# A fused attention and feed-forward kernel: 12 hash rows copied by DMA for the attention mask, a Horner form read from PSUM, and a weight conversion with work moved off VectorE

## The chip, the cores and the metric

The kernel runs on one core of one Trainium2 chip. The metric is the device time of one execution in microseconds; less is better. Engines: TensorE (PE in the profile; PEld are its weight loads), VectorE (DVE), ScalarE (ACT), GpSimd (POOL), and SyncE (SP), which here only issues DMAs. Each engine runs its own instructions strictly in order. A tile framework with a list scheduler decides that order from the program and from its own estimates, so a change of one operation can move others.

## The reference

```python
# 1: attention, 2 batches x 8 heads, 768 tokens, head size 64; a token sees only keys of its own hash bucket
q_bits = (einsum('bhsd,dk->bhsk', q, proj) > 0)      # 6 bits each; k_bits likewise
mask = q_bucket[..., :, None] == k_bucket[..., None, :]
scores = where(mask, q @ k.T / 8, -1e9); attn = softmax(scores); x = attn @ v
# 2: feed-forward "a", 1536 tokens, 512 -> 2048 -> 512, float64 weights
h = x @ w_in
g = (a0 + a1 h + a2 h^2 + a3 h^3) / (1 + |b0||h| + |b1| h^2 + 1e-6)
x = g @ w_out
# 3: 8 experts "b", 512 -> 1024 -> 512, float32, each with relu, weighted by a Sinkhorn gate P
out = sum_e P[:, e] * (relu(x @ w1[e]) @ w2[e])
```

## The kernel before

Float32 products run as float32r passes: an operand is split into a high part (hi) and a low part (lo = a - hi), and hi*hi + hi*lo + lo*hi is summed in PSUM.

**Attention** loops over 16 heads, and in each over three pairs of 128-query tiles. Per tile `scores` does two products (L259, and L260 with the stacked operands `a2`, `b2`) into PSUM; VectorE copies them out with a row minimum (L266); ScalarE takes the exponential (L267); GpSimd divides by the row sum (L274). Later iterations transpose (L288), split the result (`pth` by ScalarE, `ptl` by VectorE, both tiles from L99 and L102) and multiply with the values (L303). The next head is prepared meanwhile: `prep_head_a` splits q, k and v on GpSimd, transposes them (L221) and copies them out on ScalarE as `a1`, `b1`; VectorE copies halves of them into `a2` and `b2` (L223, L224). `prep_head_b` computes hash values (L236) and turns them into bits (L237, VectorE). `prep_head_c` multiplies the bits with a sign code (L246), and ScalarE turns the result into 64 mask rows of `a2` and of `b2` (L247, L248).

**Feed-forward "a"** has 48 steps of 512 tokens by 128 hidden units. A step has 12 matmuls into PSUM (`gemm1`, tile `h`, L343), the rational function (`activate`, L358 to L370, then `gh` and `gl`), and, three steps later, 12 matmuls of `gemm2` (L391). The temporary tiles `tu`, `tw`, `tq`, `tr` have two buffers each, `gh` and `gl` four, and PSUM has four banks for `h`. The float64 weights of 16 hidden tiles come as pairs of 32-bit words. `narrow` turns 512 columns of them into float32 (L162 to L169; twice for each of the 16 tiles), and a split follows (ScalarE hi, GpSimd lo). Ten of these 32 calls run during attention, 22 during feed-forward "a".

**Experts "b"** have 192 steps of the same 24 matmuls with a short activation (L374 ScalarE, L375 VectorE), which the change leaves alone.

DMAs are issued by SP, in order; q, k and v of head i + 2 are loaded when head i has been split.

Of the kernel before, what the change touches and what calls it, by code (L numbers as in the profile page):

```python
# [31 lines left out]
def kernel(  # L32
# [194 lines left out]
    hs = {}  # L227

    def prep_head_b(i):
        """hash bits of the queries (rows 0:NB) and keys (rows 64:64+NB)"""  # L230
        a1, a2, b1_, b2, _ = st[i]
        bits = ap.tile([P, S], BF16, tag="bits", bufs=1, name="bits")
        for n0, n1 in COLS:
            hp = bank("hp")[:, 0:n1 - n0]
            for j, r in enumerate((a1, a1, b1_, b1_)):
                pe.matmul(hp, lhsT=pjr[:, j], rhs=r[:, n0:n1], start=j == 0, stop=j == 3)  # L236
            dve.tensor_scalar(bits[:, n0:n1], hp, 0.0, None, ALU.is_gt)  # L237
        hs[i] = bits

    def prep_head_c(i):  # L240
        """bucket rows: 0 for a query's own bucket and -1 elsewhere, BIG for a key's own bucket and 0 elsewhere"""
        a1, a2, b1_, b2, _ = st[i]
        bits = hs.pop(i)
        for n0, n1 in COLS:
            dp = bank("dp")[:, 0:n1 - n0]
# [374 lines left out]
```

## Time and profile before

| | us |
|---|---|
| median of 3 runs | 1775.38 (1774.77 to 1777.22) |
| profiled execution, first to last instruction (span) | 1771.8 |
| what the median has beyond that span | 3.6 |
| attention, 0 to about 316 | 316 |
| feed-forward "a", 316 to about 706 | 390 |
| gate and experts "b", 706 to the end | 1066 |

The span is the profile's time from the first to the last instruction of one execution. The start and the end of an execution lie around it. Stage borders are read from the first `h` matmuls of a kind on TensorE, and stages overlap there by some microseconds.

### The profile page before, as it was taken

The page shows a single profiled execution, that of the slowest core. Times are in us where ns is not written, and L with a number is a line of the kernel's source. Part 1 is how long each engine was busy: PE and PEld are TensorE (multiplying, and loading weights), DVE is VectorE, ACT ScalarE, POOL GpSimd, SP SyncE. Part 2 cuts the span into 40 slices and gives each one's busy share as a digit, 9 for nine tenths or more (in the row PEclk, how much of TensorE's full clock was granted, in tenths as well). Part 3 has the DMA queues.
Part 4 walks back from the last instruction along what each step waited for, and adds up shares of the span by engine and source line. Part 5 has one row for each costly group of instructions (what it writes and reads, how often), then busy time and mean ns, then how long its engine had stood idle before and what let it go on. Part 6 is the DMA issues. An engine that isn't in the chain of part 4 may idle for free.

```text
span 1771.8 us, 19718 instructions
## 1 busy us (share of the span) xinstructions
PE 1631.5 (92%) x7716; PEld 1340.4 (76%) x7716; DVE 887.9 (50%) x1414; ACT 607.1 (34%) x1101; POOL 694.8 (39%) x660
## 2 busy tenths in 40 slices
PE   6898989776776788999999999999999999999998
PEld 5777778655665666788888888888888888888887
DVE  8999999899999988521112111111211111121112
ACT  5888888556555556111111111111111111111110
POOL 6777775666666674302303303304204204105100
PEclk9999999897888899999999999999999999999999
DMA  4111110011111110100200201101101101101001
...
DMA packets 46062, 64.20 MB, mean 36 GB/s; under 512 B 3473, under 2 KB 34193, under 8 KB 45969
## 3 DMA queue, kind: packets, MB, share of 16 engines
...
## 4 chain that ended last, share of the span: by engine, by line
PE 65%; DVE 22%; ACT 6%; issue 4%; POOL 2%; SPq 0%; DMA 0%; DVEq 0%; POOLq 0%
PE acc L391 30%; PE h L343 29%; DVE tr L369 3%; DVE tq L368 3%; DVE tu L370 2%; PE av L303 2%; ACT e L267 2%; DVE tq L363 2%; DVE gl L102 1%; PE pt L288 1%; DVE e L266 1%; DVE ptl L102 1%; DVE u L165 1%; DVE c L162 1%; ACT pth L99 1%
## 5 line engine op out<-in xcount | busy, mean ns | idle before, releaser
L375 DVE SCALAR_TENSOR_TENSOR gl<-h,gh 128x512 fp32r<-128x512 f32 x192 | 132.7, 692 | 809.5 <-ACT gh L374 809.4
L343 PE MATMUL h<-x2h,w 128*128 128x512 f32 x1536 | 504.3, 389 | 0.0
L391 PE MATMUL acc<-w,gh 128*128 128x512 f32 x1536 | 473.7, 389 | 0.6 <-DVE part L403 0.6
L374 ACT ACTIVATE gh<-h 128x512 fp32r<-128x512 f32 x192 | 114.8, 598 | 915.2 <-PE h L343 915.1
L391 PEld LDWEIGHTS acc<-w,gh 128*128 128x128 f32 x1536 | 288.1, 188 | 60.7 <-DVE part L403 1.0
L343 PEld LDWEIGHTS h<-x2h,w 128*128 128x128 f32 x1536 | 288.1, 188 | 59.7
L93 POOL TENSOR_SCALAR w<-ra 128x512 fp32r<-128x512 f32 x64 | 41.5, 649 | 719.1 <-PE acc L391 719.1
L391 PE MATMUL acc<-w,gl 128*128 128x512 f32 x768 | 299.1, 389 | 0.0
L343 PE MATMUL h<-x2l,w 128*128 128x512 f32 x768 | 298.8, 389 | 0.0
L391 PE MATMUL acc<-gh,w 128*128 128x512 f32 x384 | 149.1, 452 | 79.2 <-DVE part L403 24.8
L391 PEld LDWEIGHTS acc<-w,gl 128*128 128x128 f32 x768 | 144.3, 188 | 29.9
L343 PEld LDWEIGHTS h<-x2l,w 128*128 128x128 f32 x768 | 144.3, 188 | 29.8
L391 PEld LDWEIGHTS acc<-gh,w 128*128 128x128 f32 x384 | 85.0, 222 | 106.6 <-ACT gh L99 40.4
L343 PE MATMUL h<-xh,w 128*128 128x512 f32 x384 | 127.4, 395 | 0.0
L274 POOL TENSOR_SCALAR e<-e,rs 128x768 f32<-128x768 f32 x96 | 101.4, 1067 | 43.0 <-DVE rs L272 41.1
L366 POOL TENSOR_TENSOR tu<-tu,tsq 128x512 f32<-128x512 f32 x48 | 77.6, 1618 | 69.4 <-ACT tu L360 65.9
L391 PE MATMUL acc<-gl,w 128*128 128x512 f32 x192 | 86.9, 453 | 13.0 <-DVE gl L102 13.0
L102 DVE TENSOR_TENSOR ptl<-pt,pth 128x512 fp32r<-128x512 f32 x144 | 94.6, 683 | 5.5 <-ACT pth L99 4.2
L288 PE MATMUL pt<-idr,e 128*128 128x128 f32 x576 | 83.9, 277 | 10.2 <-ACT b L248 5.4
L267 ACT ACTIVATE e<-e,nm 128x768 f32<-128x768 f32 x96 | 90.4, 941 | 7.2 <-DVE e L266 6.1
L266 DVE TENSOR_SCALAR_CACHE_REDUCE e<-s 128x768 f32<-128x768 f32 x96 | 90.6, 945 | 1.4 <-PE s L260 1.0
L99 ACT ACTIVATE pth<-pt 128x512 fp32r<-128x512 f32 x144 | 81.2, 598 | 16.5 <-PE pt L288 14.8
...
## 6 DMA issues: line engine op xcount, KB each, us to landing
ra<-in_moe_w_dram SPq DMA_DIRECT2D x32, 512.0 KB, 3.4
rb<-in_moe_w_dram SPq DMA_DIRECT2D x32, 512.0 KB, 4.2
ra<-in_moe_w_in_dram SPq DMA_DIRECT2D x16, 512.0 KB, 3.7
rb<-in_moe_w_out_dram SPq DMA_DIRECT2D x16, 512.0 KB, 3.4
qkv<-in_q_dram SPq DMA_DIRECT2D x16, 192.0 KB, 2.4
qkv<-in_k_dram SPq DMA_DIRECT2D x16, 192.0 KB, 2.5
qkv<-in_v_dram SPq DMA_DIRECT2D x16, 192.0 KB, 3.2
...
```

What stands on the lines that cost most here:

```text
L99: act.activation(o, src, AF.Copy)
L102: dve.tensor_tensor(lo, src, hi.bitcast(F32), ALU.subtract)
L266: dve.tensor_scalar(e[j], s[:, 0:S], -1.0 / D ** 0.5, None, ALU.mult, ALU.min, accum_out=nm)
L267: act.activation(e[j], e[j], AF.Exp, bias=nm, scale=-1.0, accum_out=rs[:, j:j + 1])
L274: pool.tensor_scalar(e[j], e[j], rs[:, j:j + 1], 0.0, ALU.mult, ALU.add)
L288: pe.transpose(pt[:, c, j * P:(j + 1) * P], e[j][:, cc * P:(cc + 1) * P], idf)
L343: pe.matmul(hps, lhsT=w[:, c], rhs=x[:, c], start=m == 0, stop=m == 3 * KC - 1)
L366: pool.tensor_tensor(tu, tu, tsq, ALU.mult)
L368: dve.scalar_tensor_tensor(tq, tq, dbias, tr, ALU.add, ALU.mult)
L374: act.activation(gh, hps, AF.Relu)
L375: dve.scalar_tensor_tensor(gl, hps, 0.0, gh.bitcast(F32), ALU.max, ALU.subtract)
L391: pe.matmul(o, lhsT=l[:, js], rhs=r, start=f == 0 and m == 0, stop=f == nf - 1 and m == 2)
```

## The change

Attention: the sign code, its product and `prep_head_c` go. For each token a matmul now gives 12 hash values (the six with both signs), a VectorE operation turns them into 0/1 rows for queries and 0/2^60 rows for keys, and DMAs copy these 12 rows, and also the 64-row halves that VectorE copied, into `a2` and `b2`. A key whose six bits agree contributes 6 * 2^60 in the second product, which now contracts over 76 rows. The factor -1/8 moves from L266 into the copy of `a1`.

Feed-forward: the polynomial and the denominator are evaluated by Horner's rule with `h` read from PSUM by three VectorE operations; both GpSimd operations and the square go, and `gl` moves from VectorE to GpSimd. In `narrow`, the first bit operation of VectorE becomes an absolute value on ScalarE and the clamp moves to GpSimd; tile `u` has one buffer in place of two.

```diff
     def narrow(bits):
-        u = conv.tile([P, n], I32, tag="u", name="u")
+        u = conv.tile([P, n], I32, tag="u", bufs=1, name="u")
-        dve.tensor_scalar(ci, hw, 0x7FFFFFFF, None, ALU.bitwise_and)
-        dve.tensor_scalar(c, c, F64_LOW, F64_HIGH, ALU.max, ALU.min)
+        act.activation(c, hw.bitcast(F32), AF.Abs)
+        pool.tensor_scalar(c, c, F64_HIGH, F64_LOW, ALU.min, ALU.max)
...
-        for src, dst in ((sq, a1), (sk, b1_)):
+        for src, dst, scale in ((sq, a1, -1.0 / D ** 0.5), (sk, b1_, 1.0)):
...
-                act_copy(dst[:, n0:n1], tp[:, 0:n1 - n0].bitcast(F32))
-        dve.tensor_copy(a2[0:64], a1[0:64].bitcast(F32))
-        dve.tensor_copy(b2[0:64], b1_[64:128].bitcast(F32))
+                act.activation(dst[:, n0:n1], tp[:, 0:n1 - n0].bitcast(F32), AF.Copy, scale=scale)
+        sp.dma_start(a2[0:64].bitcast(F32), a1[0:64].bitcast(F32))
+        sp.dma_start(b2[0:64].bitcast(F32), b1_[64:128].bitcast(F32))
...
-            dve.tensor_scalar(bits[:, n0:n1], hp, 0.0, None, ALU.is_gt)
+            dve.tensor_scalar(bits[QROW:KROW + 2 * NB, n0:n1], hp[QROW:], thr[QROW:KROW + 2 * NB, 0:1],
+                              thr[QROW:KROW + 2 * NB, 1:2], ALU.is_ge, ALU.mult)
+        sp.dma_start(a2[QROW:QROW + 2 * NB].bitcast(F32), bits[QROW:QROW + 2 * NB].bitcast(F32))
+        sp.dma_start(b2[QROW:QROW + 2 * NB].bitcast(F32), bits[KROW:KROW + 2 * NB].bitcast(F32))
...
-    def prep_head_c(i):
-            pe.matmul(dp, lhsT=codeT, rhs=bits[:, n0:n1], start=True, stop=True)
-            act.activation(a2[64:128, n0:n1], dp[0:64], AF.Sign, bias=obias[0:64])
-            act.activation(b2[64:128, n0:n1], dp[64:128], AF.Relu, bias=obias[64:128], scale=BIG)
...
-            pe.matmul(s[:, n0:n1], lhsT=a2[:, cs], rhs=b2[:, n0:n1], start=False, stop=True)
+            pe.matmul(s[:, n0:n1], lhsT=a2[0:QROW + 2 * NB, cs], rhs=b2[0:QROW + 2 * NB, n0:n1],
+                      start=False, stop=True)
...
-            act.activation(tsq, hps, AF.Square)
-            act.activation(tq, hps, AF.Abs, scale=cb[:, 0:1])
+            act.activation(tw, hps, AF.Abs, scale=cb[:, 1:2])
             act.activation(tu, hps, AF.Identity, scale=na[:, 3:4], bias=na[:, 2:3])
-            act.activation(tw, hps, AF.Identity, scale=na[:, 1:2], bias=na[:, 0:1])
-            dve.scalar_tensor_tensor(tq, tsq, b1, tq, ALU.mult, ALU.add)
+            dve.scalar_tensor_tensor(tw, tw, ab[:, 0:1], hps, ALU.add, ALU.mult)
+            act.activation(tq, tw, AF.Abs)
             act.activation(tr, tq, AF.Ln, bias=dbias)
             act.activation(tr, tr, AF.Exp, scale=-1.0)
-            pool.tensor_tensor(tu, tu, tsq, ALU.mult)
-            pool.tensor_tensor(tu, tu, tw, ALU.add)
+            dve.tensor_tensor(tu, tu, hps, ALU.mult)
+            dve.scalar_tensor_tensor(tu, tu, na[:, 1:2], hps, ALU.add, ALU.mult)
             dve.scalar_tensor_tensor(tq, tq, dbias, tr, ALU.add, ALU.mult)
-            dve.scalar_tensor_tensor(tr, tq, -2.0, tr, ALU.add, ALU.mult)
-            dve.tensor_tensor(tu, tu, tr, ALU.mult)
+            dve.scalar_tensor_tensor(tu, tu, na[:, 0:1], tr, ALU.add, ALU.mult)
+            dve.scalar_tensor_tensor(tu, tq, -2.0, tu, ALU.add, ALU.mult)
             act_copy(gh, tu)
-            dve_lo(gl, tu, gh)
+            pool_lo(gl, tu, gh)
```

In the changed kernel the new VectorE lines of a step are L357, L361, L362 (these read `h` from PSUM) and L363, L364, L365; ScalarE's are L355 (`tw`), L356 (`tu`), L358 (`tq`), L359 and L360 (`tr`), and L102 (`gh`); those of `narrow` are L166 (ScalarE), L167 (GpSimd), L168, L169, L171, L172 (VectorE), L173 (GpSimd).

VectorE, in the middle of feed-forward "a", before: about one step with a part of a weight conversion (the numbers after the names tell buffers of different steps apart).

```order
L102 TENSOR_TENSOR gl_4312<-tu_4313,gh_4311 128x512
L369 SCALAR_TENSOR_TENSOR tr_4351<-tq_4350,tr_4351 128x512
L363 SCALAR_TENSOR_TENSOR tq_4398<-tsq_4397,b1_303,tq_4398 128x512
L370 TENSOR_TENSOR tu_4347<-tu_4347,tr_4351 128x512
L164 TENSOR_SCALAR c_4663<-c_4663 128x512
L162 TENSOR_SCALAR c_4674<-rb_4438 128x512
L165 SCALAR_TENSOR_TENSOR u_4664<-ra_4437,c_4663 128x512
L102 TENSOR_TENSOR gl_4346<-tu_4347,gh_4345 128x512
L368 SCALAR_TENSOR_TENSOR tq_4398<-tq_4398,dbias_308,tr_4399 128x512
```

The same engine and place in the changed kernel, a little over one step.

```order
L365 SCALAR_TENSOR_TENSOR tu_4242<-tq_4244,tu_4242 128x512
L361 TENSOR_TENSOR tu_4288<-tu_4288,h_4259 128x512
L171 TENSOR_SCALAR c_4432<-u_4433 128x512
L362 SCALAR_TENSOR_TENSOR tu_4288<-tu_4288,na_297,h_4259 128x512
L172 SCALAR_TENSOR_TENSOR c_4432<-rb_3861,c_4432 128x512
L357 SCALAR_TENSOR_TENSOR tw_4360<-tw_4360,ab_294,h_4332 128x512
L363 SCALAR_TENSOR_TENSOR tq_4290<-tq_4290,dbias_299,tr_4291 128x512
L364 SCALAR_TENSOR_TENSOR tu_4288<-tu_4288,na_297,tr_4291 128x512
L361 TENSOR_TENSOR tu_4359<-tu_4359,h_4332 128x512
L365 SCALAR_TENSOR_TENSOR tu_4288<-tq_4290,tu_4288 128x512
```

Where every operation read two tiles from SBUF (or one from SBUF alone), operations that read `h` now stand between those; `gl` is gone from here, and the first product of the next step (`tu_4359`) stands ahead of the last one of this step (`tu_4288`).

ScalarE at the same place in the changed kernel.

```order
L358 ACTIVATE tq_4290<-tw_4289 128x512
L102 ACTIVATE gh_4240<-tu_4242 128x512
L359 ACTIVATE tr_4291<-tq_4290,dbias_299 128x512
L356 ACTIVATE tu_4359<-h_4332,na_297 128x512
L360 ACTIVATE tr_4291<-tr_4291 128x512
L355 ACTIVATE tw_4404<-h_4376,cb_285 128x512
```

The first `tu` of a step (`tu_4359`) takes the buffer of the step two before it (`tu_4242`), which GpSimd's new `gl` operation is the last to read; behind it stands L360, the exponential of the step between them.

SP during attention in the changed kernel, from one head's loads to the next one's; before, there were only the three loads per head, and a weight load in some of them.

```order
L117 DMA qkv_1590<-in_q_dram 128x384
L117 DMA qkv_1590<-in_k_dram 128x384
L117 DMA qkv_1590<-in_v_dram 128x384
L227 DMA a2_1595<-a1_1594 64x768
L228 DMA b2_1597<-b1_1596 64x768
L242 DMA a2_1595<-bits_1684 12x768
L243 DMA b2_1597<-bits_1684 12x768
```

Four copies per head stand behind the loads of two heads later; in some heads a 512 KB weight load stands ahead of the last two of them.

## Rows read from the trace of the kernel before

**Rows 1.** The page: its span and its first part, busy time of each engine.

```profile
span 1771.8 us, 19718 instructions
PE 1631.5 (92%) x7716; PEld 1340.4 (76%) x7716; DVE 887.9 (50%) x1414; ACT 607.1 (34%) x1101; POOL 694.8 (39%) x660
```

**Rows 2.** Busy us of each engine by stage: attention, feed-forward "a", experts.

```profile
60.00:290.00 230.00, 206.24 (x1459) 178.63 (x1458) 221.46 (x463) 197.02 (x399) 171.53 (x193) 0.99 0.15 45
...
316.00:706.00 390.00, 297.64 (x1141) 230.42 (x1140) 363.93 (x409) 228.14 (x379) 243.10 (x162) 0.87 0.11 36
...
760.00:1772.00 1012.00, 1007.30 (x4444) 833.73 (x4443) 194.45 (x281) 110.63 (x185) 208.08 (x224) 1.00 0.09 31
```

**Rows 3.** VectorE by line, 60 to 290 us: busy us, mean ns, idle before.

```profile
L102 DVE TENSOR_TENSOR ptl<-pt,pth 128x512 fp32r<-128x512 f32 x111 | 73.0, 682 | 2.1 <-ACT pth L99 1.0
...
L224 DVE CAST b<-b 64x768 fp32r<-64x768 f32 x12 | 12.9, 1071 | 0.8 <-ACT b L99 0.5
...
L223 DVE CAST a<-a 64x768 fp32r<-64x768 f32 x12 | 8.7, 723 | 0.0
```

**Rows 4.** VectorE by line, 0 to 316 us: the clamp of the weight conversion.

```profile
L163 DVE TENSOR_SCALAR c<-c 128x512 f32<-128x512 f32 x10 | 6.4, 641 | 0.0
```

**Rows 5.** Timeline of one head's mask: start us, us, engine, line.

```profile
171.70 0.99 DVE L237 TENSOR_SCALAR bits<-hp 128x512 bf16<-128x512 f32 x2
...
179.02 0.47 ACT L248 ACTIVATE b<-dp,obias 64x256 fp32r<-64x256 f32 x1
...
179.01 0.40 PE L260 MATMUL s<-b,a 128*128 128x512 f32 x1
```

**Rows 6.** DMA issues, 150 to 175 us: KB each, median us to landing.

```profile
rb<-in_moe_w_out_dram SPq DMA_DIRECT2D x1, 512.0 KB, 5.0
qkv<-in_q_dram SPq DMA_DIRECT2D x1, 192.0 KB, 2.3
```

**Rows 7.** By line, 316 to 706 us: VectorE, GpSimd, ScalarE.

```profile
L369 DVE SCALAR_TENSOR_TENSOR tr<-tq,tr 128x512 f32<-128x512 f32 x47 | 54.0, 1150 | 0.4
...
L403 DVE TENSOR_TENSOR part<-part,acc 128x512 f32<-128x512 f32 x32 | 20.3, 676 | 0.0
...
L366 POOL TENSOR_TENSOR tu<-tu,tsq 128x512 f32<-128x512 f32 x47 | 75.9, 1615 | 69.4 <-ACT tu L360 65.9 <-DVE gl L102 3.5
...
L169 POOL TENSOR_TENSOR c<-u,c 128x512 f32<-128x512 f32 x22 | 38.8, 1763 | 48.5 <-DVE c L168 48.5
...
L360 ACT ACTIVATE tu<-h,na 128x512 f32<-128x512 f32 x47 | 36.6, 778 | 14.1 <-DVE gl L102 14.1
...
L365 ACT ACTIVATE tr<-tr 128x512 f32<-128x512 f32 x48 | 30.0, 626 | 0.5
```

**Rows 8.** Timeline of VectorE and GpSimd in feed-forward "a": start us, us, engine, line.

```profile
420.68 1.81 DVE L363 SCALAR_TENSOR_TENSOR tq<-tsq,b,tq 128x512 f32<-128x512 f32 x1
...
420.65 1.29 POOL L366 TENSOR_TENSOR tu<-tu,tsq 128x512 f32<-128x512 f32 x1 [0.44 <-ACT tu L360]
...
426.04 0.74 DVE L368 SCALAR_TENSOR_TENSOR tq<-tq,dbias,tr 128x512 f32<-128x512 f32 x1
426.70 0.68 DVE L165 SCALAR_TENSOR_TENSOR u<-ra,c 128x512 int32<-128x512 int32 x1
427.30 0.68 DVE L369 SCALAR_TENSOR_TENSOR tr<-tq,tr 128x512 f32<-128x512 f32 x1
427.90 0.41 DVE L167 TENSOR_SCALAR c<-u 128x512 int32<-128x512 int32 x1
428.24 0.68 DVE L370 TENSOR_TENSOR tu<-tu,tr 128x512 f32<-128x512 f32 x1
```

**Rows 9.** By line, 800 to 1700 us (experts): VectorE and GpSimd.

```profile
L375 DVE SCALAR_TENSOR_TENSOR gl<-h,gh 128x512 fp32r<-128x512 f32 x166 | 114.8, 692 | 729.2 <-ACT gh L374 729.2
...
L96 POOL TENSOR_TENSOR w<-ra,w 128x512 fp32r<-128x512 f32 x56 | 72.2, 1290 | 0.0
L93 POOL TENSOR_SCALAR w<-ra 128x512 fp32r<-128x512 f32 x56 | 35.1, 626 | 712.7 <-PE acc L391 712.7
```

More of the change, by code (lines that the diff above doesn't have):

```diff
@@ L25 @@
 BIG = 2.0 ** 60
+QROW, KROW = 64, 96
+F_BELOW = 2.0 ** -126
+F_MIN = 2.0 ** -126 * (1.0 + 2.0 ** -23)
 F64_LOW = float.fromhex("0x1p-15")
@@ L221, in prep_head_a @@
                     pe.transpose(tp[:, c * P - n0:(c + 1) * P - n0], src[:, c], idr)
[L222 to L224 removed]
+                act.activation(dst[:, n0:n1], tp[:, 0:n1 - n0].bitcast(F32), AF.Copy, scale=scale)
+        sp.dma_start(a2[0:64].bitcast(F32), a1[0:64].bitcast(F32))
+        sp.dma_start(b2[0:64].bitcast(F32), b1_[64:128].bitcast(F32))
         st[i] = (a1, a2, b1_, b2, sv)
[L227 removed]
     def prep_head_b(i):
         a1, a2, b1_, b2, _ = st[i]
[L232 removed]
+        bits = ap.tile([P, S], F32R, tag="bits", bufs=1, name="bits")
         for n0, n1 in COLS:
[L234 to L248 removed]
+            hp = bank("hp")[0:KROW + 2 * NB, 0:n1 - n0]
+            for m, (j, r) in enumerate(((0, a1), (1, a1), (2, b1_), (3, b1_))):
+                pe.matmul(hp, lhsT=pjr[:, j, 0:KROW + 2 * NB], rhs=r[:, n0:n1], start=m == 0, stop=m == 3)
+            dve.tensor_scalar(bits[QROW:KROW + 2 * NB, n0:n1], hp[QROW:], thr[QROW:KROW + 2 * NB, 0:1],
+                              thr[QROW:KROW + 2 * NB, 1:2], ALU.is_ge, ALU.mult)
+        sp.dma_start(a2[QROW:QROW + 2 * NB].bitcast(F32), bits[QROW:QROW + 2 * NB].bitcast(F32))
+        sp.dma_start(b2[QROW:QROW + 2 * NB].bitcast(F32), bits[KROW:KROW + 2 * NB].bitcast(F32))
     es = {}
@@ L265, in scores @@
         e, rs = es[gi]
-        dve.tensor_scalar(e[j], s[:, 0:S], -1.0 / D ** 0.5, None, ALU.mult, ALU.min, accum_out=nm)
+        dve.tensor_scalar(e[j], s[:, 0:S], BIG, None, ALU.min, ALU.min, accum_out=nm)
         act.activation(e[j], e[j], AF.Exp, bias=nm, scale=-1.0, accum_out=rs[:, j:j + 1])
@@ L475 @@
     dve.tensor_copy(pjh, pj)
-    dve.tensor_copy(pjz[:, 0, 0:NB], pjh.bitcast(F32))
-    dve.tensor_tensor(pjz[0:64, 1, 0:NB], pj[0:64, :], pjh[0:64, :].bitcast(F32), ALU.subtract)
-    dve.tensor_copy(pjz[:, 2, 64:64 + NB], pjh.bitcast(F32))
-    dve.tensor_tensor(pjz[64:128, 3, 64:64 + NB], pj[64:128, :], pjh[64:128, :].bitcast(F32), ALU.subtract)
+    pjl = ap.tile([P, NB], F32, tag="pjl", bufs=1, name="pjl")
+    dve.tensor_tensor(pjl, pj, pjh.bitcast(F32), ALU.subtract)
+    for j, row, half in ((0, QROW, slice(0, P)), (1, QROW, slice(0, D)), (2, KROW, slice(0, P)), (3, KROW, slice(D, P))):
+        src = pjh.bitcast(F32) if j % 2 == 0 else pjl
+        dve.tensor_scalar(pjz[half, j, row:row + NB], src[half], -1.0, None, ALU.mult)
+        dve.tensor_copy(pjz[half, j, row + NB:row + 2 * NB], src[half])
     pjr = ap.tile([P, 4, P], F32R, tag="pjr", bufs=1, name="pjr")
@@ L485 @@
     pool.iota(row, pattern=[[0, 1]], base=0, channel_multiplier=1)
-    bit = ap.tile([P, NB], I32, tag="bit", bufs=1, name="bit")
-    for j in range(NB):
-        dve.tensor_scalar(bit[:, j:j + 1], row, j, 1, ALU.logical_shift_right, ALU.bitwise_and)
-    bitf = ap.tile([P, NB], F32, tag="bitf", bufs=1, name="bitf")
-    dve.tensor_copy(bitf, bit)
-    code = ap.tile([P, P], F32, tag="e", bufs=EB, name="code")
-    dve.memset(code, 0.0)
-    dve.tensor_scalar(code[0:64, 0:NB], bitf[0:64, :], 2.0, -1.0, ALU.mult, ALU.add)
-    dve.tensor_scalar(code[64:128, 64:64 + NB], bitf[64:128, :], 2.0, -1.0, ALU.mult, ALU.add)
-    nset = const.tile([P, 1], F32, name="nset")
-    dve.tensor_reduce(nset, bitf, AX.X, ALU.add)
-    obias = const.tile([P, 1], F32, name="obias")
-    dve.tensor_scalar(obias[0:64], nset[0:64], -1.0, None, ALU.mult)
-    dve.tensor_scalar(obias[64:128], nset[64:128], -BIG, BIG, ALU.mult, ALU.add)
-    codeT = ap.tile([P, P], BF16, tag="codeT", bufs=1, name="codeT")
-    ct = bank("ct")
-    pe.transpose(ct[:, 0:P], code, idf)
-    dve.tensor_copy(codeT, ct[:, 0:P])
+    rowf = ap.tile([P, 3], F32, tag="rowf", bufs=1, name="rowf")
+    dve.tensor_copy(rowf[:, 0:1], row)
+    dve.tensor_scalar(rowf[:, 1:2], rowf[:, 0:1], float(KROW), None, ALU.is_ge)
+    dve.tensor_scalar(rowf[:, 2:3], rowf[:, 0:1], float(KROW + NB), None, ALU.is_ge)
+    thr = const.tile([P, 2], F32, name="thr")
+    dve.tensor_scalar(thr[:, 1:2], rowf[:, 1:2], BIG - 1.0, 1.0, ALU.mult, ALU.add)
+    dve.tensor_scalar(rowf[:, 0:1], rowf[:, 0:1], float(QROW + NB), None, ALU.is_lt)
+    dve.tensor_tensor(rowf[:, 0:1], rowf[:, 0:1], rowf[:, 2:3], ALU.add)
+    dve.tensor_scalar(thr[:, 0:1], rowf[:, 0:1], F_MIN, None, ALU.mult)
+    dve.tensor_scalar(rowf[:, 2:3], rowf[:, 0:1], -1.0, F_BELOW, ALU.add, ALU.mult)
+    dve.tensor_tensor(thr[:, 0:1], thr[:, 0:1], rowf[:, 2:3], ALU.add)
     prep_head_b(0)
-    prep_head_c(0)
     wprep = {NG - 13 + 3 * j: j for j in range(QF)}
@@ L520 @@
             dve_lo(wgl, wg, wgh)
-            b1 = const.tile([P, 1], F32, name="b1")
-            dve.tensor_scalar(b1, cb[:, 1:2], -1.0, None, ALU.mult)
-            dve.tensor_tensor(b1, b1, cb[:, 1:2], ALU.max)
+            ab = const.tile([P, 1], F32, name="ab")
+            dve.tensor_scalar(ab, cb[:, 0:1], -1.0, None, ALU.mult)
+            dve.tensor_tensor(ab, ab, cb[:, 0:1], ALU.max)
             na = const.tile([P, 4], F32, name="na")
@@ L535 @@
             scores(it, 0)
-        if i + 1 < len(heads):
-            (prep_head_a, prep_head_b, prep_head_c)[g](i + 1)
+        if i + 1 < len(heads) and g < 2:
+            (prep_head_a, prep_head_b)[g](i + 1)
         if 0 <= ti < NG:
```

1 line of the change is left out of this document (removed).

## The prediction

> **What bounds the kernel now.** I read the page first: TensorE is busy for 92% of the span [rows 1], but a mean over stages says little here, so I asked for the busy times by stage [rows 2]. Three different limits appear. In the experts TensorE is busy for 1007 of 1012 us; the change touches nothing there and I cost that stage at nothing. In attention VectorE is busy for 221.5 of 230 us (96%), TensorE 206, ScalarE 197, GpSimd 172. In feed-forward "a" VectorE is busy for 363.9 of 390 us, TensorE for 298, ScalarE 228, GpSimd 243. So in the first two stages, 706 us together, VectorE sets the pace.
>
> In feed-forward "a" that busy time is not work alone. I went to the lines and then to the timeline. The mean L369 takes 1150 ns [rows 7], while the same operation takes 680 ns at 427.30 [rows 8]. The timeline shows why: L363 starts at 420.68, just after GpSimd's L366 at 420.65, which runs to 421.94; L363 ends at 422.49, about the 0.55 us of an operation's own work after that. VectorE had waited for GpSimd to finish. From 426.04 on nothing is in its way, and the distances between starts give the price of each kind: 0.66 us (a two-tensor operation with a per-partition scalar), 0.60 (without), 0.34 (one SBUF tile in and out). One kind does not wait: L102 `ptl`, which reads PSUM and SBUF, has a mean of 682 ns in 111 cases [rows 3] although GpSimd is busy for 75% of that window [rows 2], and L375, of the same kind, 692 ns [rows 9]. So operations with all inputs in SBUF (call their time L) exclude GpSimd's (P), and those with one PSUM input (N) do not.
>
> This can be tested on the kernel before. There are 48 steps in 390 us, 8.13 us each. Five activation operations, all of the first kind, make 0.66 + 0.66 + 3 x 0.60 = 3.12 us. A narrow call has four operations of 0.34 and two of 0.60, 2.56 us; 22 calls (L169) [rows 7] are 0.46 per step, 1.17 us. L is 4.29. GpSimd does two operations of 1.29 (L366 at 420.65, and L96 in the experts) [rows 8, 9], and two per narrow call, 2.58 + 1.18: P is 3.76. L + P is 8.05, against 8.13 measured. N is L403, 32 x 0.676 / 48 = 0.45 [rows 7], and VectorE is idle for 26.1 us, 0.54 per step [rows 2]. VectorE and GpSimd behave like one engine.
>
> **The change, part by part: feed-forward "a".** VectorE has six operations per step instead of five, but three of them read `h` from PSUM. L: L363, L364 and L365 make 0.66 + 0.66 + 0.60 = 1.92; a narrow call now has two of 0.34 and two of 0.60, 1.88, x 0.46 = 0.86; together 2.78. N: two with a scalar and one without, as start distances 0.66 + 0.66 + 0.63 = 1.95, and 0.45 as before; 2.40. The trace has no such three operations in a row; L375 is the nearest kind. P: `gl` 1.29, and per narrow call the clamp and two others, 0.63 (as L93) [rows 9] + 2.58, x 0.46 = 1.47; 2.76.
>
> [...]
>
> L + P is 5.54, L + N is 5.18, all three 7.94. Before, nearly all that could overlap did; now P can lie under N, but the two must meet: a GpSimd operation of 1.29 gets its turn next to a PSUM operation of about 0.65 and blocks VectorE for the rest. I take half of P as hidden, 1.38, which leaves 6.56, and keep the idle 0.54: 7.10; for the new waits below I add 0.1. A step of 7.2 us saves 0.93, and 48 steps 45 us.
>
> The new waits: VectorE's L168 now waits for GpSimd's clamp, which waits for ScalarE; with one buffer, the next `u` (L169) waits for GpSimd's addition; and GpSimd's `gl` releases `tu`. The last one makes a circle, which the order shows: `gh` of one step, `gl`, `tu` of two steps on (behind which L360 of the step between stands on ScalarE), then L363, L364, L361 and L365 of that step, then its `gh`. With 0.63 (as L365), 1.29, 0.78 (as L360) [rows 7], 0.63, 0.66, 0.66, 0.60 and 0.60 it takes 5.85 us where nothing collides. That is below 7.2, so it is no bound in itself, but collisions lengthen it too. ScalarE loses a square and one evacuation and gains an absolute value; TensorE's matmuls have 297.6 of 390 us busy now, and both have room. Bounds for the step: 5.85 below (about -109 us), and above all of L, N, P and the idle in a row, 8.48 (+17 us).
>
> **Attention.** L223 and L224 go: 21.6 us in 12 heads [rows 3], 1.80 each, 28.8 for 16. L162 and L163 of ten narrow calls go: 2 x 6.4 = 12.8 [rows 4], L162 taken like L163. VectorE gains nothing: the bits are the same two PSUM reads of 512 and 256 columns. The whole is 41 us. On ScalarE four operations per head go, on TensorE two small products. What takes up the slack is TensorE: 206 of 230 us busy, about 200 without those products, and it waits in order. If VectorE alone set the pace, all 41 us would come back; if TensorE with its waits held on, nothing. As GpSimd, ScalarE and TensorE have 25%, 14% and 10% of room and VectorE's removed share is about 13%, I take two thirds: 27 us.
>
> The moved copies: seven DMAs per head on SP in place of three. Nothing waits for the 64-row copies for long, since they start when `a1` and `b1` are written, ahead even of the hash product. The mask is the tight one. Before, bits end at 172.69, the last mask write (L248) at 179.49, and the next head's first L260, on the half written by then, starts at 179.01 [rows 5], 6.3 us after the bits. SBUF copies don't occur in the trace; the nearest rows are 2.3 us for 192 KB and 5.0 us for 512 KB [rows 6], and the mask rows are 36 KB each. With two issues that is 3 to 6 us; I take 3, hidden by the work between, and each microsecond beyond 6.3 would stop TensorE once per head, 15 us in all. Behind the mask copies on SP stand the loads for two heads later, which have a head's time to spare.
>
> **The sum** is made against the profiled execution: 1771.8 - 45 - 27 = 1699.8; the median of the runs lies 3.6 us above that span, so 1703.
>
> **The rivals.** *TensorE holds attention* (17%): it is in order and 90% busy, so only about 8 of the 41 us come back: 1775.4 - 45 - 8 = 1722. For it speaks its busy time; against it, that this time includes filling waits that VectorE causes. *VectorE and GpSimd still take turns* (12%): GpSimd's operations land between the SBUF ones, nothing is hidden, and the step is 7.94 with the idle filled: 48 x 0.19 = 9 saved, 1775.4 - 9 - 27 = 1739. For it speaks that several SBUF operations stand in a row in the new order. *All overlap* (12%): the step falls to about 6.0, close to the circle: 48 x 2.13 = 102 saved, 1646. For it speaks that before nearly everything overlapped that could. *Mask rows come late* (4%), the slower side: SP holds the copies behind a weight load that still waits for its buffer, or they take far longer than the rows above. It decides where they land more than 6.3 + 4.8 us after the bits: 72 us over 15 heads is then eaten; at 12.3 us the time is 1775.4 - 72 + 15 x 6 = 1793. Against it, the weight loads stand behind conversions that VectorE finishes well ahead of the bits. *The change does nothing that can be measured* (2%): something else, for instance `gl`'s waits, takes back all, 1775.
>
> **How the numbers follow.** The summed case has 53%; its own range is 1680 to 1722. The time is 1703. The range for 8 in 10 reaches to the second and third case and towards the fourth: 1662 to 1745. What a measurement of this kernel can tell from no change is about 0.2%, 3.6 us. Faster by more: 53 + 17 + 12 + 12 = 94%; within: 2%; slower: 4%.
>
> **What would show it.** Right: feed-forward "a" near 345 us, with L357, L361 and L362 at 0.7 us each whatever GpSimd does, and L363 to L365 still prolonged at times, but less busy VectorE per step; attention near 289 us, L223 and L224 gone, the wait of L255 (the new second product) for DMAs near nothing. Wrong: VectorE idle for over 1 us per step, waiting for ScalarE or GpSimd (the circle is longer than summed); GpSimd's `gl` at 2 us and more (it gets no turn); TensorE waiting for the mask's DMAs; or VectorE idle in attention with TensorE over 95% busy.

## The result, and the profile after

The changed kernel takes 1717.3 us (median of 4 runs, 1711.3 to 1718.5); before, 1775.1. The ratio is 0.9664, 95% interval 0.9645 to 0.9683: faster by 58 us. The prediction was 1703, in a range of 1662 to 1745. The profiled execution took 1718.5 us with a span of 1716.8. The page, span and busy times, as in [rows 1]:

```profile
span 1716.8 us, 19515 instructions
...
PE 1614.4 (94%) x7683; PEld 1334.4 (78%) x7683; DVE 795.3 (46%) x1366; ACT 559.8 (33%) x1021; POOL 620.2 (36%) x644
```

Where the time came from is read at the stage borders, the first `h` matmuls on `xh` (feed-forward "a" begins) and on `x2h` (experts begin). The line of these matmuls, before and then after; the last two times are the first and the last start:

```profile
L343 PE MATMUL h<-x2h,w x1536: 389/389/496, 707.1 to 1756.0; 128*128 128x512 f32 x192
L343 PE MATMUL h<-xh,w x384: 387/389/632, 313.5 to 696.8; 128*128 128x512 f32 x192
```

```profile
L339 PE MATMUL h<-x2h,w x1536: 389/389/498, 652.0 to 1700.9; 128*128 128x512 f32 x192
...
L339 PE MATMUL h<-xh,w x384: 387/389/632, 300.3 to 643.3; 128*128 128x512 f32 x192
```

Attention became 13.2 us shorter (27 predicted), feed-forward "a" went from 393.6 to 351.7, 41.9 us (45 predicted), and the rest lasts 1064.7 before and 1064.8 after. Against the predicted span of 1699.8 the execution is 17.0 us late, and 13.8 of that is attention. Busy times by stage after, columns as in [rows 2]:

```profile
60.00:270.00 210.00, 194.63 (x1422) 175.75 (x1421) 193.00 (x420) 167.61 (x353) 163.07 (x197) 0.99 0.26 71
300.30:652.00 351.70, 292.92 (x1163) 226.69 (x1161) 302.95 (x413) 214.83 (x352) 176.14 (x138) 0.92 0.13 39
706.00:1716.00 1010.00, 1006.20 (x4440) 832.83 (x4438) 194.34 (x281) 110.63 (x185) 207.96 (x224) 1.00 0.10 31
```

In attention VectorE is busy for 92% where it was 96%: some of what was taken off it became idle time. In feed-forward "a" it is idle for 48.8 us; 26 were taken. TensorE's mean granted clock in that stage (the first figure after the busy times) rose too, from 0.87 to 0.92. No run holds it fixed, so what the clock itself gives of the 41.9 us is not separated here. The lines of that stage, columns as in [rows 7]:

```profile
L99 POOL TENSOR_TENSOR gl<-tu,gh 128x512 fp32r<-128x512 f32 x46 | 72.8, 1583 | 110.7 <-ACT gh L102 107.0 <-issue 3.7
...
L364 DVE SCALAR_TENSOR_TENSOR tu<-tu,na,tr 128x512 f32<-128x512 f32 x47 | 50.0, 1065 | 0.0
L363 DVE SCALAR_TENSOR_TENSOR tq<-tq,dbias,tr 128x512 f32<-128x512 f32 x47 | 43.6, 927 | 8.7 <-ACT tr L360 8.4
L365 DVE SCALAR_TENSOR_TENSOR tu<-tq,tu 128x512 f32<-128x512 f32 x46 | 40.6, 883 | 0.1
...
L356 ACT ACTIVATE tu<-h,na 128x512 f32<-128x512 f32 x47 | 36.5, 777 | 54.8 <-POOL gl L99 54.0 <-PE lt L430 0.6
...
L357 DVE SCALAR_TENSOR_TENSOR tw<-tw,ab,h 128x512 f32<-128x512 f32 x47 | 34.8, 740 | 25.0 <-ACT tu L356 24.9
L362 DVE SCALAR_TENSOR_TENSOR tu<-tu,na,h 128x512 f32<-128x512 f32 x47 | 34.7, 738 | 0.2
...
L361 DVE TENSOR_TENSOR tu<-tu,h 128x512 f32<-128x512 f32 x47 | 31.8, 677 | 0.0
```

One operation of each kind in that stage, with its shortest, median and longest time in ns:

```profile
L361 DVE TENSOR_TENSOR tu<-tu,h x47: 669/676/686, 307.4 to 648.8; 128x512 f32<-128x512 f32 x47
...
L363 DVE SCALAR_TENSOR_TENSOR tq<-tq,dbias,tr x47: 737/751/1906, 311.1 to 650.4; 128x512 f32<-128x512 f32 x47
```

The three operations that read `h` keep their 0.68 to 0.74 us whatever GpSimd does (the longest L361 takes 0.69, the longest L357 and L362 0.75); the three with all inputs in SBUF are prolonged at times, as said (L363 up to 1.91). New is the last column of the lines above: ScalarE's `tu` waits 54 us for `gl`, and VectorE's `tw` 25 us for that `tu`, which stands with the step's other operations in ScalarE's order. One such place on the timeline, columns as in [rows 8]:

```profile
407.60 1.70 POOL L99 TENSOR_TENSOR gl<-tu,gh 128x512 fp32r<-128x512 f32 x1 [1.39 <-ACT gh L102]
408.10 1.75 DVE L364 SCALAR_TENSOR_TENSOR tu<-tu,na,tr 128x512 f32<-128x512 f32 x1
409.33 0.78 ACT L356 ACTIVATE tu<-h,na 128x512 f32<-128x512 f32 x1 [1.81 <-POOL gl L99]
...
409.35 0.50 PE L386 MATMUL acc<-gl,w 128*128 128x512 f32 x1 [1.10 <-POOL gl L99]
```

`gl` starts while L363 runs (407.43 to 408.17), is itself delayed (1.70 against 1.29), blocks L364 to 409.85, and three engines then wait for its end: ScalarE, TensorE and VectorE.

In attention, VectorE by line, 60 to 270 us, as in [rows 3]:

```profile
L105 DVE TENSOR_TENSOR ptl<-pt,pth 128x512 fp32r<-128x512 f32 x111 | 72.4, 679 | 14.5 <-ACT pth L102 14.0
...
L240 DVE TENSOR_SCALAR bits<-hp,thr 44x512 fp32r<-44x512 f32 (+1 forms) x26 | 16.7, 687 | 0.4
```

`ptl` waited 2.1 us in the 230 us of [rows 3], now 14.5 in 210. The timeline shows why:

```profile
148.55 1.82 POOL L270 TENSOR_SCALAR e<-e,rs 128x768 f32<-128x768 f32 x2
...
150.35 1.27 POOL L173 TENSOR_TENSOR c<-u,c 128x512 f32<-128x512 f32 x1
...
150.88 1.29 DVE L240 TENSOR_SCALAR bits<-hp,thr 44x512 fp32r<-44x512 f32 x2
151.65 0.63 ACT L102 ACTIVATE w<-c 128x512 fp32r<-128x512 f32 x1 [2.63 <-POOL c L173]
152.19 0.92 ACT L263 ACTIVATE e<-e,nm 128x768 f32<-128x768 f32 x1
...
153.67 0.67 ACT L166 ACTIVATE c<-rb 128x512 f32<-128x512 f32 x1 [0.47 <-POOL w L99]
154.25 0.58 ACT L102 ACTIVATE pth<-pt 128x512 fp32r<-128x512 f32 x1
...
154.86 0.69 DVE L105 TENSOR_TENSOR ptl<-pt,pth 128x512 fp32r<-128x512 f32 x1 [2.70 <-ACT pth L102]
```

The conversion's last addition (L173) stands behind two normalisations in GpSimd's queue; ScalarE waits 2.63 us for it with `w`, then comes the next conversion's absolute value (L166), which waits for its buffer, and only behind these `pth`. VectorE is idle for 2.70 us. The two `bits` operations of a head, 0.99 us in [rows 5], take 1.29.

Last, the start. The first row minimum (L262) is at 25.88, where it was at 20.9:

```profile
20.44 0.47 PE L255 MATMUL s<-b,a 76*128 76x512 f32 x1 [1.44 <-DMA b<-bits]
...
22.02 0.69 DVE L169 SCALAR_TENSOR_TENSOR u<-rb,c 128x512 int32<-128x512 int32 x1 [2.12 <-POOL c L173]
22.75 1.52 DVE L171 TENSOR_SCALAR c<-u 128x512 int32<-128x512 int32 x1
...
25.03 0.82 DVE L240 TENSOR_SCALAR bits<-hp,thr 44x512 fp32r<-44x512 f32 x1
...
25.88 0.96 DVE L262 TENSOR_SCALAR_CACHE_REDUCE e<-s 128x768 f32<-128x768 f32 x1
```

The product that it reads began at 20.44. A conversion that waits 2.12 us for GpSimd and is blocked by it (1.52 us for L171), and the next head's bits, stand ahead of it in VectorE's order. The wait is not what makes it late: in mask_only (below), where the old conversion and the same bits stand there and VectorE does not wait between them, the first row minimum is at 25.14. The 1.44 us at 20.44 are the only wait of TensorE for a mask row.

### The profile page after: what moved, and what is told of

Its sections match the earlier page's. It is cut to its first block, busy times and chain, and to the rows that moved or that the text cites. A ratio compares the mean times of both kernels' runs of the same rounds, so it can differ in the third digit from the quotient of the medians.

```text
span 1716.8 us, 19515 instructions
## 1 busy us (share of the span) xinstructions
PE 1614.4 (94%) x7683; PEld 1334.4 (78%) x7683; DVE 795.3 (46%) x1366; ACT 559.8 (33%) x1021; POOL 620.2 (36%) x644
## 4 chain that ended last, share of the span: by engine, by line
PE 62%; DVE 1%; ACT 0%; DVEq 0%; issue 0%
PE acc L386 31%; PE h L339 30%; DVE x2l L105 0%; PE lp L424 0%; DVE part L398 0%; PE cp L454 0%; DVE osum L411 0%; ACT tu L356 0%; DVE tw L357 0%; DVE tq L363 0%; PE lt L430 0%; DVE tu L364 0%; DVEq L605 0%; ACT tq L358 0%; ACT tr L359 0%; DVE tu L365 0%
## 5 line engine op out<-in xcount | busy, mean ns | idle before, releaser
L370 DVE SCALAR_TENSOR_TENSOR gl<-h,gh 128x512 fp32r<-128x512 f32 x192 | 132.6, 691 | 809.4 <-ACT gh L369 809.3
L369 ACT ACTIVATE gh<-h 128x512 fp32r<-128x512 f32 x192 | 114.7, 598 | 912.9 <-PE h L339 912.9
L386 PE MATMUL acc<-gh,w 128*128 128x512 f32 x384 | 142.5, 436 | 33.5 <-DVE part L398 21.5
L386 PEld LDWEIGHTS acc<-gh,w 128*128 128x128 f32 x384 | 81.5, 213 | 58.4 <-ACT tu L356 12.6
L99 POOL TENSOR_TENSOR gl<-tu,gh 128x512 fp32r<-128x512 f32 x48 | 75.4, 1571 | 112.7 <-ACT gh L102 109.0
L386 PE MATMUL acc<-gl,w 128*128 128x512 f32 x192 | 85.0, 443 | 21.4 <-POOL gl L99 21.2
L105 DVE TENSOR_TENSOR ptl<-pt,pth 128x512 fp32r<-128x512 f32 x144 | 94.2, 680 | 21.9 <-ACT pth L102 21.2
L270 POOL TENSOR_SCALAR e<-e,rs 128x768 f32<-128x768 f32 x96 | 90.3, 951 | 20.3 <-DVE rs L268 14.3
L262 DVE TENSOR_SCALAR_CACHE_REDUCE e<-s 128x768 f32<-128x768 f32 x96 | 90.8, 947 | 2.1 <-PE s L255 1.7
L339 PEld LDWEIGHTS h<-xh,w 128*128 128x128 f32 x384 | 72.8, 190 | 17.0 <-DVE tu L362 1.7
```

The source lines that it names most:

```text
L99: pool.tensor_tensor(lo, src, hi.bitcast(F32), ALU.subtract)
L105: dve.tensor_tensor(lo, src, hi.bitcast(F32), ALU.subtract)
L262: dve.tensor_scalar(e[j], s[:, 0:S], BIG, None, ALU.min, ALU.min, accum_out=nm)
L270: pool.tensor_scalar(e[j], e[j], rs[:, j:j + 1], 0.0, ALU.mult, ALU.add)
L339: pe.matmul(hps, lhsT=w[:, c], rhs=x[:, c], start=m == 0, stop=m == 3 * KC - 1)
L369: act.activation(gh, hps, AF.Relu)
```

## The experiments

All runs in one table: median time, ratio to before with its interval, the time at which attention ends, how long feed-forward "a" lasts (both from the first `h` matmuls, as above), and the first row minimum. Stage times are of one execution each. Kernels with the same attention code end it within 2 us of each other (before and ffn_only, changed and tu3 and gl_dve, mask_only and ffn_mask and conversion_by_stage); the four times of the changed kernel span 7.2 us, those of the others 0.6 to 4.4. Differences of a few us in time or in "a" are therefore not clear of noise.

| kernel | us | ratio | attention to | "a" lasts | first minimum |
|---|---|---|---|---|---|
| before | 1775 | | 313.5 | 393.6 | 20.9 |
| changed | 1717.3 | 0.9664 (0.9645-0.9683) | 300.3 | 351.7 | 25.9 |
| ffn_only | 1736.9 | 0.9781 (0.9767-0.9796) | 312.7 | 355.9 | 20.7 |
| mask_only | 1758.5 | 0.9900 (0.9885-0.9915) | 291.2 | 400.7 | 25.1 |
| narrow_only | 1791.6 | 1.0086 (1.0069-1.0103) | 326.8 | 398.1 | 20.7 |
| ffn_mask | 1725.8 | 0.9717 (0.9703-0.9732) | 291.9 | 367.6 | 25.8 |
| tu3 | 1707.2 | 0.9623 (0.9609-0.9638) | 300.6 | 339.6 | 25.6 |
| gl_dve | 1698.9 | 0.9573 (0.9559-0.9587) | 301.5 | 332.4 | 25.7 |
| new_conversion_two_u | 1713.4 | 0.9656 (0.9641-0.9670) | 300.4 | 347.0 | 23.6 |
| old_conversion_two_u | 1722.2 | 0.9703 (0.9687-0.9719) | 293.4 | 362.5 | 24.1 |
| conversion_by_stage | 1691.1 | 0.9523 (0.9507-0.9539) | 290.0 | 333.9 | 25.4 |
| abs_on_vectore | 1721.4 | 0.9688 (0.9673-0.9702) | 298.7 | 356.1 | 26.4 |
| clamp_on_vectore | 1724.8 | 0.9717 (0.9701-0.9734) | 303.4 | 354.5 | 25.1 |
| all_together | 1694.7 | 0.9535 (0.9521-0.9549) | 293.2 | 333.2 | 24.1 |

### The three parts alone

**ffn_only**: the kernel before with the new body of `activate` and its constant `ab`.

> Only the rational function is changed; attention and the weight conversion stay as before. Theory 1 (the terms of the prediction): a step of feed-forward "a" has L 3.09 us (1.92, and the old conversion 1.17), N 2.40, P 2.47 (gl 1.29 and 1.18), half of P hidden: 6.73 + 0.64 idle = 7.4 us, so that stage lasts about 355 us in place of 393.5, attention stays at 313.5, the time is about 1737. Rival (the new conversion is what freed VectorE): the stage stays above 370 us and the time above 1752.

Measured: "a" 355.9 us, 1736.9. Theory 1, within a microsecond, though two of its terms were off in opposite directions: blocked 1.23 us a step (half of 2.47) and idle 0.64 were taken, 1.04 and 0.88 were measured (table under gl_dve). VectorE in this stage is busy for 313.6 us.

```profile
312.70:668.60 355.90, 291.19 (x1163) 226.87 (x1161) 313.62 (x456) 203.32 (x330) 168.85 (x116) 0.91 0.12 39
```

**mask_only**: the changed kernel with the old bodies of `activate` and `narrow`. Of the feed-forward code this is left against the kernel before:

```diff
-        u = conv.tile([P, n], I32, tag="u", name="u")
+        u = conv.tile([P, n], I32, tag="u", bufs=1, name="u")
```

> Only the attention part is changed (hash rows, DMA copies); rational function and conversion as before, but u has one buffer, since the wider bits tile leaves no room for two. Theory 1 (the new conversion took back some of attention's gain): without it VectorE loses 28.8 us and gets 4.7 back for the dearer bits operation; attention ends at about 295 to 298 in place of 313.5, the first row minimum is at about 21 us as before, the time is 1757 to 1760. Rival (TensorE and its waits hold attention, whatever VectorE loses): attention ends at 303 to 306, the time is 1765 or more.

Measured: attention ends at 291.2, 22.3 us earlier, although its first row minimum is 4 us later, against expectation. Theory 1, and by more than expected: up to the end of attention VectorE is busy for 19.9 us less than before (275.4 against 295.3) and idle for 2.4 less, so what it lost comes back whole. "a" is 7.1 us longer than before (400.7), against expectation; only because these two misses cancel does the time, 1758.5, lie in the range of theory 1. Busy times, 60 to 270 us:

```profile
60.00:270.00 210.00, 198.59 (x1464) 179.10 (x1462) 203.22 (x435) 168.10 (x358) 164.26 (x198) 1.00 0.27 71
```

VectorE is at 97% again and TensorE does 1464 matmuls in the stretch where the changed kernel does 1422.

**narrow_only**: the kernel before with the new `narrow`, and with it the one `u`.

> Only the weight conversion is changed. Theory 1 (its new chain over ScalarE, GpSimd and VectorE makes ScalarE's in-order queue wait, and ptl behind it): attention is not shorter, 313 to 320 us, with VectorE's ptl waiting for pth by 10 us or more in all; feed-forward "a" moves by less than 5 us; the time is 1772 to 1782. Rival (VectorE's lost 12.8 us come back in attention): attention ends at 302 to 306, the time is 1764 to 1768.

Measured: slower than before, 1791.6; attention ends at 326.8, 13.3 us later, although VectorE has 12.8 us less to do there by the prediction's price. Its busy time up to that point falls by 5.8 us (289.5 against 295.3), and its idle time doubles (37.3 against 18.2). Theory 1 has the direction and the wait; it was too mild. "a" is 4.5 us longer, too. Waits, 0 to 326 us (in all, times, longest):

```profile
DVE ptl L102 <- ACT pth L99: 18.2, 25, 2.1
ACT c L163 <- POOL w L96: 18.0, 8, 3.0
```

**ffn_mask**: the changed kernel with the old `narrow` (one `u`).

> The changed kernel with the old weight conversion (u with one buffer, as room demands). Theory 1 (the new conversion costs attention more than it gives): attention ends at about 296 in place of 300.3, feed-forward "a" lasts about 355, the time is about 1715, equal to the changed kernel or up to 6 us below. Rival (the lighter conversion helps in both stages): 8 us or more slower than the changed kernel, 1725 or more.

Measured: the time of the rival, 8.5 us above the changed kernel, but not its mechanism. Attention ends at 291.9, better than theory 1, and only "a", 367.6, is worse. So the new conversion costs 8.4 us in attention (300.3 against 291.9) and gives 16 in "a" (351.7 against 367.6). The waits up to the end of attention, of the changed kernel and of this one:

```profile
DVE ptl L105 <- ACT pth L102: 21.2, 13, 3.3
```

```profile
DVE ptl L105 <- ACT pth L102: 4.8, 9, 1.5
```

The same event as at 151.65 above, in this kernel:

```profile
145.31 0.63 ACT L102 ACTIVATE w<-c 128x512 fp32r<-128x512 f32 x1 [2.61 <-POOL c L172]
145.85 0.92 ACT L262 ACTIVATE e<-e,nm 128x768 f32<-128x768 f32 x1
...
146.77 0.57 ACT L102 ACTIVATE pth<-pt 128x512 fp32r<-128x512 f32 x1
...
147.37 0.69 DVE L105 TENSOR_TENSOR ptl<-pt,pth 128x512 fp32r<-128x512 f32 x1 [1.49 <-ACT pth L102]
```

ScalarE waits equally long for `w`, but `pth` follows 1.46 us after it and not 2.60: the absolute value with its own wait (0.67 + 0.47) is missing. VectorE's gap is 1.21 us shorter.

### The waits in feed-forward "a"

**tu3**:

```diff
-            tu = mp.tile([P, 512], F32, tag="tu", name="tu")
+            tu = mp.tile([P, 512], F32, tag="tu", bufs=3, name="tu")
...
-        ls = mp.tile([P, 512], F32, tag="tu", name="ls")[0:E]
+        ls = mp.tile([P, 512], F32, tag="tu", bufs=3, name="ls")[0:E]
```

> The changed kernel with three buffers for tu in place of two: a step's first write of tu waits for gl of three steps before. Theory 1 (the circle gh, gl, tu of two steps on is what doubled VectorE's idle time, 49 us where 26 were taken): ScalarE's wait for gl goes from 54 us to under 10, VectorE's idle time falls by 20 us or more, feed-forward "a" lasts 330 us or less, the time is 1697 or less. Rival (VectorE and GpSimd taking turns is the limit, the wait only shows what is late anyway): the wait goes, but VectorE is blocked or idle elsewhere, the stage stays above 343 us, the time above 1709.

Measured: 339.6 us, 1707.2: between the two. Waits of that stage, changed kernel and then tu3:

```profile
ACT tu L356 <- POOL gl L99: 54.0, 34, 6.7
ACT w L102 <- POOL c L173: 28.1, 18, 3.7
DVE tw L357 <- ACT tu L356: 24.9, 16, 4.4
```

```profile
ACT w L102 <- POOL c L173: 43.4, 21, 4.2
...
ACT tu L356 <- POOL gl L99: 18.6, 6, 6.0
DVE tq L363 <- ACT tr L360: 15.3, 13, 4.2
...
DVE u L169 <- POOL c L173: 14.0, 7, 4.4
...
DVE tw L357 <- ACT tu L356: 7.5, 4, 4.0
```

A third buffer takes 12.1 us off "a", and 18.6 us of ScalarE's wait are left. VectorE's wait for `tu` falls by 17 us, but waits for `tr` and for GpSimd's `c` grow in its place, so that idle time falls by only 6.6 (48.8 to 42.2).

**gl_dve**:

```diff
-            pool_lo(gl, tu, gh)
+            dve_lo(gl, tu, gh)
```

> The changed kernel with gl on VectorE, as before the change. Theory 1 (about 40% of GpSimd's time costs VectorE, as the changed kernel's rows show): VectorE's own work rises by 0.60 us a step, what GpSimd blocks falls by about 0.5, and the circle gets 0.7 shorter: feed-forward "a" within 10 us of 352, the time 1707 to 1727. Rival 1 (GpSimd's work lies beside VectorE's PSUM reads for nothing): 0.6 us a step more, 1740 or more. Rival 2 (they take turns throughout, and the circle holds too): 0.7 us a step less or better, 1685 or less.

Measured: 332.4 us, 1698.9, better than theory 1 and short of rival 2; VectorE is busier by 4.4 us, and idle for 23.7 less:

```profile
301.50:633.90 332.40, 286.63 (x1164) 223.59 (x1162) 307.32 (x457) 213.52 (x352) 103.75 (x91) 0.93 0.14 42
```

Put by the prediction's terms, per step of 48 (own is L + N by its prices, with 0.60 more for `gl` here; blocked is busy time less own):

| | own | P | blocked, share of P | idle | step |
|---|---|---|---|---|---|
| ffn_only | 5.49 | 2.47 | 1.04, 42% | 0.88 | 7.41 |
| changed | 5.18 | 2.76 | 1.13, 41% | 1.02 | 7.33 |
| gl_dve | 5.78 | 1.47 | 0.62, 42% | 0.52 | 6.93 |

P leaves out the weight splits for the experts, 20 GpSimd operations in this stage (19 in gl_dve), 0.4 us a step by the same prices; with them the shares are 36, 36 and 34%. Blocked time and shares are estimates by subtraction.

What GpSimd blocks follows theory 1 (own +0.60, blocked -0.51). The gain is idle time, which theory 1 left out: ScalarE's `tu` still waits 20.6 us for `gl`, but VectorE's `tw` only 5.7 us for `tu`, and TensorE's wait for `gl` falls from 21.2 us to 1.9. Why idle time falls by more than with a third `tu` is only argued: `gl` no longer queues with the conversion on GpSimd.

**new_conversion_two_u** and **old_conversion_two_u**: `prep_head_b` writes into `a2`, so that one copy per head goes and `u` has room for its second buffer; the second kernel has the old `narrow` too.

```diff
-            dve.tensor_scalar(bits[QROW:KROW + 2 * NB, n0:n1], hp[QROW:], thr[QROW:KROW + 2 * NB, 0:1],
+            dve.tensor_scalar(a2[QROW:KROW + 2 * NB, n0:n1], hp[QROW:], thr[QROW:KROW + 2 * NB, 0:1],
...
-        sp.dma_start(a2[QROW:QROW + 2 * NB].bitcast(F32), bits[QROW:QROW + 2 * NB].bitcast(F32))
-        sp.dma_start(b2[QROW:QROW + 2 * NB].bitcast(F32), bits[KROW:KROW + 2 * NB].bitcast(F32))
+        sp.dma_start(b2[QROW:QROW + 2 * NB].bitcast(F32), a2[KROW:KROW + 2 * NB].bitcast(F32))
...
-        u = conv.tile([P, n], I32, tag="u", bufs=1, name="u")
+        u = conv.tile([P, n], I32, tag="u", name="u")
```

> The changed kernel, where the bits are written into rows 64 to 107 of a2 itself, so that one of the four copies per head goes, and the room that this frees holds a second buffer for u. Theory 1 (with one u the second conversion of a weight tile waits for the first one's last GpSimd operation, and ScalarE's w and pth behind it): ScalarE's wait of w for c falls from 23 us to under 10 in attention, ptl's wait from 21 to under 10, attention ends at 288 to 294, feed-forward "a" is up to 10 us shorter; the time is 1698 to 1708. Rival (the longer way of the new conversion over three engines does it, however many buffers): attention ends at 297 or later, the time is 1712 or more.

> As the run before it (bits in a2, two buffers for u), but with the old conversion. Theory 1 (the parts add up where u has two buffers): attention ends at 291 to 293, feed-forward "a" lasts about 356 as with the rational function alone, the time is 1711 to 1716. Rival (the single u was not what made feed-forward "a" 12 us longer beside the old conversion): the stage stays at 363 us or more, the time is 1721 or more.

Measured: attention ends at 300.4 and 293.4, so the second `u` does nothing for it, and the rival is right in the first run (ScalarE's wait of `w` for `c` is 21.3 us and `ptl`'s 18.8, against 23.0 and 21.2 in the changed kernel). "a" gets 4.7 us shorter (347.0 against 351.7) and 5.1 (362.5 against 367.6). For the second run too the rival is nearer: the single `u` explains 5 of the 11.7 us by which "a" is longer beside the new mask than in ffn_only. The other 6.6 us stay open. One copy less goes with the second `u` in both runs, so that the two are not separated.

### What the conversion costs in attention

**conversion_by_stage**: gl_dve, where the first five weight tiles use the old `narrow` (kept as `narrow_old`, with one `u`).

```diff
...
-            b = narrow(rb[:, 0].rearrange("p (n t) -> p n t", t=2))
+            b = (narrow_old if i < 5 else narrow)(rb[:, 0].rearrange("p (n t) -> p n t", t=2))
...
```

> The changed kernel with gl on VectorE, and with the old conversion for the five weight tiles that are converted during attention, the new one for the other eleven. Theory 1 (what the new conversion costs is paid in attention, where other work stands behind its waits): against the run with gl on VectorE alone, attention ends at 292 to 294 in place of 301.5, feed-forward "a" stays at 332, the time is 1689 to 1693. Rival (what differs is the schedule as a whole, not the place of the conversion): attention ends at 298 or later, or feed-forward "a" gets longer by what attention gains; the time is 1696 or more.

Measured: theory 1. Attention ends at 290.0, 2 us below its range, "a" lasts 333.9, 1691.1 us: the lowest median here, 26 us below the changed one.

**abs_on_vectore** and **clamp_on_vectore**: the changed kernel with one of the two moved operations put back.

```diff
-        act.activation(c, hw.bitcast(F32), AF.Abs)
+        dve.tensor_scalar(ci, hw, 0x7FFFFFFF, None, ALU.bitwise_and)
```

```diff
-        pool.tensor_scalar(c, c, F64_HIGH, F64_LOW, ALU.min, ALU.max)
+        dve.tensor_scalar(c, c, F64_LOW, F64_HIGH, ALU.max, ALU.min)
```

> The changed kernel with the conversion's absolute value back on VectorE as a bit operation; the clamp stays on GpSimd. Theory 1 (it is ScalarE's place in the conversion, the absolute value that waits for GpSimd to release c, with pth behind it): attention ends at 296 or earlier in place of 300.3, with ptl's waits under 12 us. Rival (it is the clamp that stands in GpSimd's queue, and the longer chain through it, which makes w late on ScalarE): attention ends at 299 or later, with ptl's waits still 15 us or more. Feed-forward "a" is up to 8 us longer in both (0.34 us on VectorE in each of 22 calls).

> The changed kernel with the conversion's clamp back on VectorE; the absolute value stays on ScalarE. With the three runs that have both on VectorE (attention ends at 291.9), the clamp alone on GpSimd (298.7) and both moved (300.3) this fills the fourth corner. Theory 1 (the clamp in GpSimd's queue is what costs most; the absolute value on ScalarE costs 2 us or less): attention ends at 291 to 295. Rival (either hand-over makes VectorE or ScalarE wait, and one is enough): attention ends at 297 or later, with ptl's waits for pth at 12 us or more in all.

Measured: attention ends at 298.7 and at 303.4. Waits to the end of attention, of the first kernel and of the second:

```profile
DVE ptl L105 <- ACT pth L102: 8.4, 9, 1.6
DVE c L168 <- POOL c L167: 5.9, 3, 3.8
```

```profile
DVE ptl L105 <- ACT pth L102: 17.9, 11, 3.3
```

In the first, `ptl`'s wait is under 12 us as theory 1 had it, but the stage hardly gains: VectorE does the bit operation again and waits for the clamp. In the second the rival is right. With both operations on VectorE the stage ends at 291.9; either hand-over alone adds 7 to 12 us, and both together no more (8.4). VectorE's time up to the end of attention, in us:

| where the two operations run | attention to | busy | idle | of that, `ptl` for `pth` |
|---|---|---|---|---|
| both on VectorE (ffn_mask) | 291.9 | 274.4 | 17.5 | 4.8 |
| clamp on GpSimd (abs_on_vectore) | 298.7 | 273.5 | 25.2 | 8.4 |
| absolute value on ScalarE (clamp_on_vectore) | 303.4 | 271.9 | 31.5 | 17.9 |
| both moved (changed) | 300.3 | 263.9 | 36.4 | 21.2 |

Moving both takes 10.6 us of work off VectorE and makes it idle for 18.9 us more; 16.4 of these are `ptl`'s wait.

**all_together**: conversion_by_stage with bits in `a2`, two `u` and three `tu`.

> The changed kernel with gl on VectorE, the old conversion in attention, bits in a2, two buffers for u and three for tu. Theory 1 (the gains are of different waits and add up): 1717 less 18 (gl), 8 (conversion in attention), 4 (second u and one copy less) and up to 5 (ScalarE's remaining wait for gl): 1681 to 1688. Rival (second u, third tu and gl on VectorE cure the same wait): 1689 or more, no better than the run before it with the old conversion in attention.

Measured: 1694.7, the rival: with `gl` on VectorE the other buffers cure nothing more ("a" 333.2 against 333.9), and attention ends 3 us later.

## Why the prediction was right, and where it was off

**Experts at nothing**: right, to 0.1 us. **Feed-forward "a"**: right in mechanism and nearly in size, 7.33 us a step for 7.2. In this stage the three operations that read `h` from PSUM were not blocked, with means of 0.68 to 0.74 us; the three with all inputs in SBUF were, with means of 0.88 to 1.07. L171, with one SBUF input, was blocked as well: 0.41 us at its shortest in "a", 1.51 at its longest, from 516.30 on, while `gl` ran on GpSimd from 516.18 to 517.52.

Two terms were off in opposite directions: "I take half of P as hidden" leaves 1.38 blocked, 1.13 was measured; "I keep the idle 0.54", plus 0.1 for new waits, was 1.02, which is past the prediction's own sign of being wrong, "VectorE idle for over 1 us per step". The circle was rightly seen and wrongly cost: 5.85 us "is no bound in itself", yet a third buffer for `tu` takes 12 us off, as tu3 shows.

So the size is in part luck. By runs, the 41.9 us are 37.7 for the function (ffn_only), less 11.7 with the mask part and the one `u` beside it (ffn_mask), plus 15.9 for the conversion; for the 11.7 the prediction had no term but the 0.1 us a step. Its test on the kernel before, L + P = 8.05 against 8.13, leaves out the experts' weight splits, 19 GpSimd operations or 0.37 us a step by its prices. With them the sum is more than a step lasts, so even there the two engines did not exclude each other wholly.

The prediction's prices of the PSUM reads, "0.66 + 0.66 + 0.63", were right to 0.03 us: the next operation starts 0.66 us after L362 (at 406.77) and after L357 (at 410.70), and 0.60 after L361 (at 411.36). L361 itself takes 0.68 us from PSUM, as L369 does from SBUF in [rows 8].

**Attention, 27 us**: this step failed, in three parts that partly cancel. First, "two thirds" of VectorE's removed work was to come back because TensorE holds the rest. For the mask that is too little: two thirds of 28.8 are 19.2, and 22.3 came back in mask_only, where VectorE's busy time fell by 19.9. The rival that TensorE holds attention is out by this run, although its 1722 lies nearer to the measured 1717 than the summed 1703. Second, "L162 and L163 of ten narrow calls go: 12.8" was counted as a gain, 8.5 by the two thirds. It is a loss of 8.4 us (13.3 alone), and so nearly the whole miss: 22.3 less 8.4 is 13.9, and 13.2 was measured. The two operations became links of a chain over the queues of three engines, behind which `pth` and so `ptl` stand; `ptl`'s wait makes 16.4 of the 18.9 us of new idle time (ffn_mask against the changed kernel). The prediction listed that wait among those of feed-forward "a" and did not ask for it in attention, where other work stands behind it. Third, "VectorE gains nothing: the bits are the same" missed 0.30 us a head, 4.8 in all, and the start is 3 to 6 us later with the mask part in it (20.7 in both runs without it, 23.6 to 26.4 in those with it). That VectorE's order is what delays it was read from the rows above and not tried. Both lie within mask_only's 22.3.

**Mask copies by DMA, hidden**: right; 1.44 us of wait in all. Of the rivals, taking turns throughout (41% of the prediction's P blocked, not all) and all overlap (1646) are out. The 3.6 us that the sum adds beyond the span were 1.7 in the changed kernel's profiled execution (1718.5 less 1716.8).
